# V's tiles on ScalarE's DMA queue, K's on SyncE's, in a decode block whose time is set by the transfers

## The chip, the cores and the metric

The kernel runs on one core of a Trainium2 chip. The metric is the time of one execution on the device in microseconds (us), as the median of several runs of the same program. The engines are named as the profile names them: PE is TensorE (PEld its weight loads), DVE is VectorE, ACT is ScalarE, POOL is GpSimd, SP is SyncE. An engine's name with a q behind it (SPq, ACTq, PEq) is its instruction queue: DMA issues and loop control stand there.

## The reference

One decode step of a transformer block for a batch of 2, one token each: layer norm, attention of 32 heads over a cache of 8192 keys and values, output projection, a second layer norm, and a gated MLP.

```python
def _A_ref(x, k_cache, v_cache, wq, wo):          # x: 2 x 1 x 512; caches: 2 x 32 x 8192 x 128
    q = (x @ wq) ... one row of 128 for each head
    scores = einsum("bhqd,bhkd->bhqk", q, k) * Dh ** -0.5
    o = einsum("bhqk,bhkd->bhqd", softmax(scores), v)
    return o.reshape(B, Sq, Hq * Dh) @ wo
h = x + _A_ref(_layernorm(x), A_k_cache, A_v_cache, A_wq, A_wo)
h2 = h + _B_ref(_layernorm(h), W_gate, W_up, W_down)   # (relu-gated gate * up) @ W_down, F = 1376
```

All inputs are bf16. The two caches are 134 MB each and every byte of them is used once; the weights are some 12 MB.

## The kernel before, in words

The work is cut into N = 32 steps. A step i is one batch element and two heads: its K tile is 128 partitions x 16384 bf16 (4 MB; partitions 0 to 63 hold one head, 64 to 127 the other, 128 keys of 128 numbers in each partition), its V tile has the same shape. K has two buffers (the halves of kbuf), V has two (vbuf0, vbuf1); step i uses buffer i % 2. All engines but GpSimd run in the order in which the program is written (manual_schedule), and waits on semaphores are added for each buffer that is overwritten.

scores(i) writes step i down, and the end of step i - 1 with it:

- VectorE multiplies the K tile in place with the query (L358), folds the 128 products of each key in halves (L383, four adds), sums the last eight (L387), and takes the maximum of each partition (L395).
- TensorE spreads that maximum over the partitions (L397, tile mx). It stands in TensorE's program behind the products of the step before.
- One step later, powers(i): VectorE takes the minimum of the negated maxima (L312), ScalarE the exponentials (L315, two instructions with their accumulators), into pgz.
- values(i): TensorE multiplies pgz with the V tile, 32 products of 128x8 with 128x512: in a hardware loop (L434 to L440) for i < 29, written out (products, L408) for steps 29 and 30, and the other way round (L420, 128 small products) for step 31. Step 30's are cut in two: 24 (FRONT) before the maximum of step 31, 8 behind it.
- collect(i): ScalarE copies the product from PSUM (L450). turn and normalise gather four steps at a time.

So in the order of the program, scores(i) is: the multiply of step i; powers(i - 1); values(i - 1); the loads; collect(i - 1); the folds of step i; the maximum and its matmul.

The loads are in load_kv (L140 to L148, the DMA at L144). Before the steps, SyncE issues Wq, K0 in four pieces, K1 and V0. In scores(i), for i from 1 to 30, it issues K(i + 1), which waits for VectorE to finish step i - 1 in the same buffer, and then V(i), which waits for TensorE to finish the products of step i - 2. A ring is the queue of transfers that one issuing engine has handed to the DMA engines; SyncE's is q1 in the profile, ScalarE's is q10. All loads of the kernel before are in q1, except the two rows of A_x, which ScalarE issues at the very start (L168). single_packet is set for the tiles of steps 1 to 27 (TOGETHER = 28).

Behind the steps SyncE issues V31 (L472), then Wo in three pieces (L480), W_gate and W_up (L489), W_down in three pieces (L493) and its remainder (L498). W_gate, W_up and most of W_down go into K's buffer 0 when step 30 has left it. The second and third piece of W_down wait on SyncE for V30 and for V31 to land, since they use the semaphores of those transfers again, and the remainder waits likewise for the first piece of Wo. After the last step come the output projection (L535), the second layer norm, gate and up (L571), down (L604) and the store (L618).

Of the kernel before, what the change touches and what calls it, by code (L numbers as in the profile page):

```python
# [13 lines left out]
def _free(t, offset, dims):  # L14

    return bass.AP(tensor=t.tensor, offset=t.offset + offset, ap=[t.ap[0]] + [list(d) for d in dims])


def _dram(t, offset, dims):
    return bass.AP(tensor=t.tensor, offset=t.offset + offset, ap=[list(d) for d in dims])  # L20
# [3 lines left out]
def kernel(  # L24
# [13 lines left out]
    nc = tc.nc  # L38
# [53 lines left out]
    vbuf = [big.tile([P, ROW], bf16, name=f"vbuf{s}") for s in range(2)]  # L92
# [44 lines left out]

    FRONT = 24

    def load_kv(cache, buf, i, pieces=1):  # L140
        b, g = steps[i]
        w = ROW // pieces
        for k in range(pieces):
            nc.sync.dma_start(  # L144
                out=buf[i % 2][:, k * w:(k + 1) * w],
                in_=_dram(cache, (b * Hkv + 2 * g) * Sk * Dh + k * w, [[ROW, P], [1, w]]),
                single_packet=0 < i < TOGETHER,
            )  # L148
# [15 lines left out]
    with tc.manual_schedule(engines=ORDERED):  # L164
# [128 lines left out]
        def normalise(i):  # L293
            b, g0, n = divided[i]
            c = slice(2 * g0, 2 * (g0 + n))
            rz = small.tile([P, 2 * NG], f32, tag="rz")
            nc.vector.reciprocal(out=rz[:, c], in_=o_of(i)[:, 1, c])  # L297
            nc.vector.tensor_tensor(out=ocol[:, c, b], in0=o_of(i)[:, 0, c], in1=rz[:, c], op=ALU.mult)
# [6 lines left out]
        def powers(i):  # L305
            b, g = steps[i]
            s = i % 2
            mx_ps, scol = mx.pop(i)
            if i % AGAIN == 0:
                cols["nm"] = small.tile([P, AGAIN, 2], f32, tag="nm", name="nm")  # L310
            nm = cols["nm"][:, i % AGAIN, :]
            nc.vector.tensor_reduce(out=nm, in_=mx_ps, axis=AXIS.X, op=ALU.min)  # L312
            for j in range(2):
                r = slice(j * HALF, (j + 1) * HALF)
                nc.scalar.activation(  # L315
                    out=_free(pgz[s][r, :], j, [[2, NT]]), in_=scol[r, :], func=ACT.Exp, scale=SCALE,
                    bias=nm[r, j:j + 1], accum_out=zc[r, b, g, j:j + 1],
                )

        def scores(i):  # L320
            b, g = steps[i]
            s = i % 2
            kt = kbuf[:, s, :]
            npe = NPE if i == N - 1 else 0
            nmul = NT - npe
            nv = nmul - NACT[i == N - 1]

            if i % AGAIN == 0:
                cols["scol"] = small.tile([P, AGAIN, NT], f32, tag="scol", name="scol")
            scol = cols["scol"][:, i % AGAIN, :]  # L330
            if npe:
                sc_ps = ps.tile([P, NPE, 2], f32, tag="sc")
                kT = small.tile([P, NPE * P], bf16, tag="kT")

                def times_q(c0):
                    for t in range(c0, c0 + TPC):
                        nc.tensor.matmul(
                            out=sc_ps[:, t, :], lhsT=kT[:, t * P:(t + 1) * P], rhs=_free(qT, b, [[B, 2]]),
                            start=True, stop=True,
                        )  # L340

                for c0 in range(0, NPE, TPC):
                    t_ps = ps2.tile([P, TPC, P], bf16, tag="tp")
                    for k in range(TPC):
                        t = nmul + c0 + k
                        nc.tensor.transpose(t_ps[:, k, :], kt[:, t * Dh:(t + 1) * Dh], ident)
                    nc.scalar.activation(
                        out=kT[:, c0 * P:(c0 + TPC) * P], in_=t_ps.rearrange("p t s -> p (t s)"), func=ACT.Copy,
                    )
                    if c0:  # L350
                        times_q(c0 - TPC)
                times_q(NPE - TPC)
                nc.scalar.activation(out=scol[0:HALF, nmul:NT], in_=sc_ps[0:HALF, :, 0], func=ACT.Copy)
                nc.scalar.activation(out=scol[HALF:P, nmul:NT], in_=sc_ps[HALF:P, :, 1], func=ACT.Copy)

            for t0, n in ([(0, NT // 2), (NT // 2, nmul - NT // 2)] if i == 0 else [(0, nmul)]):
                kv = _free(kt, t0 * Dh, [[Dh, n], [1, Dh]])
                nc.vector.tensor_tensor(  # L358
                    out=kv, in0=kv, in1=_free(qrep, (b * NG + g) * Dh, [[0, n], [1, Dh]]), op=ALU.mult,
                )  # L360

            left = waiting[:]
            if i >= 1:
                powers(i - 1)
            if i >= 1:
                values(i - 1)
                tc.no_sync_barrier()
                if i < N - 1:
                    load_kv(A_k_cache, kh, i + 1)
                    load_kv(A_v_cache, vbuf, i)  # L370
            for t in range(nv, nmul):
                whole = small.tile([P, Dh], f32, tag="whole")
                nc.scalar.activation(
                    out=whole, in_=kt[:, t * Dh:(t + 1) * Dh], func=ACT.Copy, accum_out=scol[:, t:t + 1],
                )
            if i >= 1:
                if i < N - 1:
                    collect(i - 1)
            width = Dh
            while width > 8:  # L380
                half = width // 2
                lo = _free(kt, 0, [[Dh, nv], [1, half]])
                nc.vector.tensor_tensor(  # L383
                    out=lo, in0=lo, in1=_free(kt, half, [[Dh, nv], [1, half]]), op=ALU.add,
                )
                width = half
            nc.vector.tensor_reduce(  # L387
                out=scol[:, 0:nv], in_=_free(kt, 0, [[Dh, nv], [1, 8]]), axis=AXIS.X, op=ALU.add,
            )

            for e in left:
                waiting.remove(e)
                normalise(e)
            pm = small.tile([P, 1], f32, tag="pm")
            nc.vector.tensor_reduce(out=pm, in_=scol, axis=AXIS.X, op=ALU.max)  # L395
            mx_ps = ps.tile([P, 2, HALF], f32, tag="mx")
            nc.tensor.matmul(  # L397
                out=mx_ps.rearrange("p a b -> p (a b)"), lhsT=_free(pm, 0, [[0, P]]), rhs=nscale,
                start=True, stop=True,
            )  # L400
            mx[i] = mx_ps, scol
            if 1 <= i < COLS:
                turn(i - 1)
# [10 lines left out]
        def values(i):  # L414
            s = i % 2
            if i >= COLS:
                sums(i)
                g = steps[i][1]
                for t in range(NT):
                    nc.tensor.matmul(  # L420
                        out=o_of(i)[:, 0, 2 * g:2 * g + 2],
                        lhsT=vbuf[s][:, t * Dh:(t + 1) * Dh], rhs=pgz[s][:, 2 * t:2 * t + 2],
                        start=(t == 0), stop=(t == NT - 1),
                    )
                    if t == NT // 2:
                        turn(i - 1)
                return

            made[i] = ps.tile([P, T4 * Dh], f32, tag="po", name="po")
            if i >= LOOPED:  # L430
                products(i, 0, FRONT if i == N - 2 else NT // T4)
                return

            with tc.tile_critical(sync_engine=PE):  # L434
                products(i, 0, LOOP)

                at = {PE: LOOP_AT} if i == 0 else None
                with nc.Fori(1, NT // T4 // LOOP, 1, engines=[PE], head_slot=at) as w:
                    for u in range(LOOP):
                        nc.tensor.matmul(  # L440
                            out=made[i][0:2 * T4, :],
                            lhsT=pgz[s][:, bass.ds((w * LOOP + u) * (2 * T4), 2 * T4)],
                            rhs=vbuf[s][:, bass.ds((w * LOOP + u) * (T4 * Dh), T4 * Dh)],
                            start=False, stop=True, skip_group_check=True,
                        )


        def collect(i):
            _, k = group(i)
            nc.scalar.activation(  # L450
                out=ob[32 * k:32 * k + 2 * T4, :], in_=made.pop(i)[0:2 * T4, :], func=ACT.Copy,
            )
# [14 lines left out]
        for i in range(N - 1):  # L467
            scores(i)
            if i + EARLY < NG // 2:
                make_q(i + EARLY)  # L470
# [176 lines left out]
```

## Time and profile before

| | |
|---|---|
| median of 3 runs | 659.16 us (659.12 to 659.32) |
| profiled execution, first to last instruction (span) | 657.6 us |
| what the median is above that span | 1.5 us |
| VectorE busy | 607.9 us (92%) |
| TensorE busy | 398.7 us (61%) |
| ScalarE busy | 67.0 us (10%) |
| read from HBM | 281.05 MB, 427 GB/s over the span |
| V tile: issue to landing, median | 23.4 us |
| K tile: issue to landing, median | 19.8 us |

The runs are whole executions; the span is that of the one execution that was profiled, and the profile gives no other time for it. A slice row of the page divides the span into 40 equal parts of 16.4 us; a digit is the busy share in tenths. In a timeline a line gives the start and the length in us, the engine, the source line, the operation, the tile written and the tiles read, how many of them were merged, and in brackets how long the engine had been idle and for whom. A landing is the moment at which the last of the 16 DMA engines has reported its share of a transfer. The trace also holds one record for each packet: start, duration, size and queue. A full row of a K or V tile is one such record of 32768 bytes.

### The profile page before, as it was taken

To read this page: it belongs to the slowest core of one execution; us is meant where nothing else is said; L and a number is where in the kernel's file an instruction comes from. 1 tells how busy PE (TensorE), PEld (TensorE's weight loads), DVE (VectorE), ACT (ScalarE), POOL (GpSimd) and SP (SyncE) were. 2 spreads that over 40 slices of the span, in tenths; PEclk is the share of its full clock that TensorE was granted. 3 is DMA by queue.
4 is the path that set the end of the run, shared out by engine and by line. 5 is a ranking of instruction groups with operands and counts; after the bars stand their busy time and mean duration, and the time that the engine had idled before them with its cause. 6 is when DMAs were issued, how large, how long until landed. Compare 5 with 4: busy or idle time off the path is not lost.

```text
span 657.6 us, 7128 instructions
## 1 busy us (share of the span) xinstructions
PE 398.7 (61%) x1647; PEld 129.5 (20%) x1647; DVE 607.9 (92%) x290; ACT 67.0 (10%) x200; POOL 7.9 (1%) x51
## 2 busy tenths in 40 slices
PE   2127666666676555657666556775556665565496
PEld 1002111211121111211112111121112111121256
DVE  0899999999999999999999999999999999999941
ACT  2110111110000000000000000000000000000220
POOL 4000000000000000000000000000000000000000
PEclk9999788798887777898887789767778876779885
DMA  8999999999999999999999999999999999999997
GB/s 359 439 444 421 442 433 427 444 415 446 427 434 433 427 442 425 440 434 427 440 424 441 429 435 432 429 440 424 440 431 432 438 423 441 432 433 436 425 422 298
DMA packets 11379, 281.26 MB, mean 428 GB/s; under 512 B 1282, under 2 KB 1380, under 8 KB 2020
## 3 DMA queue, kind: packets, MB, share of 16 engines
q1 hardware_dynamic: 11360, 281.06, 99.3%
q8 instruction: 9, 0.15, 0.1%
q14 instruction: 6, 0.05, 0.0%
q10 hardware_dynamic: 4, 0.00, 0.0%
HBM read 281.05 MB, written 0.00 MB: 427 GB/s over the span
## 4 chain that ended last, share of the span: by engine, by line
DVE 61%; DMA 36%; PE 1%; issue 1%; SPq 0%; ACT 0%; DVEq 0%; ACTq 0%
DMA kbuf<-in_A_k_cache_dram 30%; DVE kbuf L358 28%; DVE kbuf L383 27%; DVE scol L387 4%; DMA vbuf<-in_A_v_cache_dram 3%; DMA kbuf<-in_B_W_down_dram 3%; PE po L408 1%; DVE nm L312 1%; DVE pm L395 0%; SPq L144 0%; ACT pgz L315 0%; PE d_ps L604 0%; SPq L166 0%; DVE rz L297 0%; PE y_ps L612 0%
## 5 line engine op out<-in xcount | busy, mean ns | idle before, releaser
L440 PE MATMUL po<-vbuf,pgz 128*8 x870 | 300.1, 443 | 68.0 <-issue 66.7
L358 DVE TENSOR_TENSOR kbuf<-kbuf,qrep 128x16384 bf16<-128x16384 bf16 (+2 forms) x33 | 277.1, 8398 | 10.2 <-DMA kbuf<-in_A_k_cache_dram 9.8
L383 DVE TENSOR_TENSOR kbuf<-kbuf 128x8192 bf16<-128x8192 bf16 (+4 forms) x128 | 274.5, 2144 | 3.3
L440 PEld LDWEIGHTS po<-vbuf,pgz 128*8 x870 | 79.9, 92 | 299.1 <-issue 263.9
L408 PE MATMUL po<-vbuf,pgz 128*8 128x512 bf16 x122 | 47.0, 521 | 135.4 <-PEq L434 111.3
L450 ACT ACTIVATE ob<-po 8x512 f32<-8x512 f32 x31 | 18.2, 586 | 436.5 <-PEq L434 427.3
L387 DVE TENSOR_REDUCE scol<-kbuf 128x128 f32<-128x1024 bf16 (+1 forms) x32 | 38.8, 1214 | 1.2
L315 ACT ACTIVATE pgz<-scol,nm 64x128 bf16<-64x128 f32 x64 | 28.0, 438 | 85.4 <-DVE nm L312 84.5
L397 PE MATMUL mx_ps<-nscale,pm 128*128 128x128 f32 x64 | 15.0, 317 | 29.7 <-DVE pm L395 19.0
L408 PEld LDWEIGHTS po<-vbuf,pgz 128*8 128x8 bf16 x58 | 2.7, 84 | 130.4 <-issue 130.4
L397 PEld LDWEIGHTS mx_ps<-nscale,pm 128*128 128x128 f32 x64 | 9.7, 190 | 39.6 <-issue 19.3
L234 PE MATMUL q_ps<-wbig,xn 128*2 128x512 bf16 x32 | 10.7, 469 | 3.0 <-DMA wbig<-in_A_wq_dram 3.0
L315 ACT ACTIVATION_READ_ACCUMULATOR pgz<-scol,nm 64x1 f32 x64 | 11.7, 184 | 0.0
L312 DVE TENSOR_REDUCE nm<-mx_ps 128x2 f32<-128x128 f32 x32 | 9.1, 284 | 1.4 <-PE mx_ps L397 1.4
L408 PEld LDWEIGHTS <-pgz 128*8 128x8 bf16 x64 | 6.1, 98 | 21.3 <-ACT pgz L315 10.0
L395 DVE TENSOR_REDUCE pm<-scol 128x1 f32<-128x128 f32 x32 | 9.1, 286 | 1.1
L459 PE MATMUL o_ps<-sel,ob 128*128 128x8 f32 (+1 forms) x64 | 8.7, 262 | 0.1
L459 PEld LDWEIGHTS o_ps<-sel,ob 128*128 128x128 f32 x64 | 8.0, 197 | 1.4 <-ACT ob L450 1.2
L215 DVE COPY xc<-x_ps 128x8 f32<-128x8 f32 x1 | 0.2, 167 | 8.4 <-PE x_ps L211 8.4
L238 ACT ACTIVATE qrow<-q_ps 2x512 bf16<-2x512 f32 x8 | 4.7, 587 | 29.5 <-PE q_ps L234 29.5
L242 PE MATMUL r_ps<-qrow,pick 2*64 2x256 bf16 x32 | 3.9, 321 | 5.4 <-ACT qrow L238 5.4
L297 DVE RECIPROCAL rz<-o_ps 128x32 f32<-128x32 f32 (+3 forms) x4 | 1.0, 254 | 5.8 <-PE o_ps L289 4.6
(93 smaller groups left out, 75.5 us busy)
## 6 DMA issues: line engine op xcount, KB each, us to landing
vbuf<-in_A_v_cache_dram SPq DMA_DIRECT2D x32, 4096.0 KB, 23.4
kbuf<-in_A_k_cache_dram SPq DMA_DIRECT2D x31, 4096.0 KB, 19.8
wbig<-in_A_wq_dram SPq DMA_DIRECT2D x1, 4096.0 KB, 12.6
kbuf<-in_A_k_cache_dram SPq DMA_DIRECT2D x4, 1024.0 KB, 17.5
wbig<-in_A_wo_dram SPq DMA_DIRECT2D x1, 2048.0 KB, 24.5
wbig<-in_A_wo_dram SPq DMA_DIRECT2D x2, 1024.0 KB, 26.4
kbuf<-in_B_W_gate_dram SPq DMA_DIRECT2D x1, 1376.0 KB, 31.2
kbuf<-in_B_W_up_dram SPq DMA_DIRECT2D x1, 1376.0 KB
```

The costliest lines, as they stand in the source:

```text
L234: nc.tensor.matmul(out=q_ps[0:B, :], lhsT=xn[:, c, :], rhs=wq_sb[:, c, n * 512:(n + 1) * 512], start=(c == 0), stop=(c == KC - 1),)
L312: nc.vector.tensor_reduce(out=nm, in_=mx_ps, axis=AXIS.X, op=ALU.min)
L315: nc.scalar.activation(out=_free(pgz[s][r, :], j, [[2, NT]]), in_=scol[r, :], func=ACT.Exp, scale=SCALE, bias=nm[r, j:j + 1], accum_out=zc ...
L358: nc.vector.tensor_tensor(out=kv, in0=kv, in1=_free(qrep, (b * NG + g) * Dh, [[0, n], [1, Dh]]), op=ALU.mult,)
L383: nc.vector.tensor_tensor(out=lo, in0=lo, in1=_free(kt, half, [[Dh, nv], [1, half]]), op=ALU.add,)
L387: nc.vector.tensor_reduce(out=scol[:, 0:nv], in_=_free(kt, 0, [[Dh, nv], [1, 8]]), axis=AXIS.X, op=ALU.add,)
L395: nc.vector.tensor_reduce(out=pm, in_=scol, axis=AXIS.X, op=ALU.max)
L397: nc.tensor.matmul(out=mx_ps.rearrange("p a b -> p (a b)"), lhsT=_free(pm, 0, [[0, P]]), rhs=nscale, start=True, stop=True,)
L408: nc.tensor.matmul(out=made[i][0:2 * T4, :], lhsT=pgz[s][:, u * 2 * T4:(u + 1) * 2 * T4], rhs=vbuf[s][:, u * T4 * Dh:(u + 1) * T4 * Dh], s ...
L440: nc.tensor.matmul(out=made[i][0:2 * T4, :], lhsT=pgz[s][:, bass.ds((w * LOOP + u) * (2 * T4), 2 * T4)], rhs=vbuf[s][:, bass.ds((w * LOOP ...
L450: nc.scalar.activation(out=ob[32 * k:32 * k + 2 * T4, :], in_=made.pop(i)[0:2 * T4, :], func=ACT.Copy,)
L459: nc.tensor.matmul(out=o_of(i)[:, 0, 2 * g0:2 * (g0 + n)], lhsT=ob[:, t * Dh:(t + 1) * Dh], rhs=sel[:, t, 0:n, :], start=(t == 0), stop=(t ...
```

## The change

load_kv takes the issuing engine as an argument. In the loop V's tiles (V1 to V30) are issued by ScalarE, at the same place of the program: on ScalarE that is behind the exponentials of step i - 1 (L315) and ahead of the copy of step i - 1 (L450). K's tiles, V0, V31 and the weights stay with SyncE.

```diff
-    def load_kv(cache, buf, i, pieces=1):
+    def load_kv(cache, buf, i, pieces=1, by=None):
         b, g = steps[i]
         w = ROW // pieces
         for k in range(pieces):
-            nc.sync.dma_start(
+            (by or nc.sync).dma_start(
                 out=buf[i % 2][:, k * w:(k + 1) * w],
                 in_=_dram(cache, (b * Hkv + 2 * g) * Sk * Dh + k * w, [[ROW, P], [1, w]]),
                 single_packet=0 < i < TOGETHER,
             )
...
                 if i < N - 1:
                     load_kv(A_k_cache, kh, i + 1)
-                    load_kv(A_v_cache, vbuf, i)
+                    load_kv(A_v_cache, vbuf, i, by=nc.scalar)
```

The programs of TensorE and VectorE are the same row for row. ScalarE's has 30 more rows, the V issues; they are gone from SyncE's.

## The prediction

> **What bounds the kernel now.** I read the slices of the page first, then the DMA part, then one period of the loop in the timeline, then the tail.
>
> ```profile
> DVE  0899999999999999999999999999999999999941
> DMA  8999999999999999999999999999999999999997
> GB/s 359 439 444 421 442 433 427 444 415 446 427 434 433 427 442 425 440 434 427 440 424 441 429 435 432 429 440 424 440 431 432 438 423 441 432 433 436 425 422 298
> ...
> q1 hardware_dynamic: 11360, 281.06, 99.3%
> ...
> DVE 61%; DMA 36%; PE 1%; issue 1%; SPq 0%; ACT 0%; DVEq 0%; ACTq 0%
> ```
>
> VectorE and the DMA engines are both full from the second slice to the last two, and one queue, q1 (SP's), carries nearly all bytes. Which of the two decides? A table by stage gives a DMA share of 1.00 and 433 GB/s from 40 to 596 us. The packet records say the same: a row of 32 KB (one partition of a K or V tile) takes 1.213 us, and the next one starts 1.209 us after it on the same engine. A 4 MB tile is 128 rows on 16 engines, 8 each: 8 x 1.209 = 9.67 us. A step moves two tiles: 19.33 us. VectorE's step, from one multiply (L358) to the next, is 19.02 us before 246 us (37.92 to 56.94). So the transfers are the slower of two almost equal chains: VectorE catches up by 0.3 us a step and from 246 us on waits for K, which the chain of waits shows as K transfers. One such period:
>
> ```profile
> 265.95 0.33 SPq L144 DMA_DIRECT2D kbuf<-in_A_k_cache_dram  x1
> 271.71 0.33 SPq L144 DMA_DIRECT2D vbuf<-in_A_v_cache_dram  x1
> 285.19 0.33 SPq L144 DMA_DIRECT2D kbuf<-in_A_k_cache_dram  x1
> 290.94 0.33 SPq L144 DMA_DIRECT2D vbuf<-in_A_v_cache_dram  x1
> ```
>
> ```profile
> 275.89 0.44 ACT L315 ACTIVATE pgz<-scol,nm 64x128 bf16<-64x128 f32 x1
> 276.19 0.18 ACT L315 ACTIVATION_READ_ACCUMULATOR pgz<-scol,nm 64x1 f32 x1
> 291.01 0.59 ACT L450 ACTIVATE ob<-po 8x512 f32<-8x512 f32 x1 [14.63 <-PEq L434]
> ```
>
> ```profile
> 285.84 8.69 DVE L358 TENSOR_TENSOR kbuf<-kbuf,qrep 128x16384 bf16<-128x16384 bf16 x1 [0.36 <-DMA kbuf<-in_A_k_cache_dram]
> ```
>
> K is issued when VectorE has finished with its buffer (265.95), V when TensorE has (271.71). By the records of landings, the V issued before (252.66) lands at 276.09, this K at 285.75, this V at 295.39: one after the other, 9.65 us apart, in the order of issue. K lands just in time: the multiply at 285.84 had waited 0.36 us.
>
> **The change, part by part.**
>
> *Instructions.* 30 V issues (V1 to V30) leave SP's program for ScalarE's; TensorE's and VectorE's programs stay row for row the same. SP gains nothing: V's wait there ends 5.7 us after K's issue, and the next K is due 13.5 us later, so no K stood behind a V. On ScalarE a V issue costs about 0.33 us (SP's row) and stands between the exponentials (L315, done at 276.37) and the copy of L450, which waits 14.6 us for TensorE anyway. Cost: nothing.
>
> *V's issue becomes later.* It now follows the exponentials: 276.4 instead of 271.7, 10.4 us after K's issue instead of 5.8. Cover: this K is served from 276.1 to 285.8, so the engines have 9 us of work. The thinnest cover is at V1: issued near 47.9 (end of the first L315 pair) instead of 38.1, while K2 is served until 52.15. From issue to first packet the first transfer took 1.0 to 1.9 us, so some 2 us remain. If a cover failed, the hole would be lost outright. Value: 0.
>
> *V's new waits* are for the earlier tile of its own buffer, read by TensorE long before, and for TensorE's loop two steps back, which L450 has already waited for. Value: 0.
>
> *Two rings share the engines.* This is what counts, and the kernel before has it only in miniature. (a) The second row of A_x is a ScalarE transfer on queue 10 in the middle of wq's stream: its 1 KB packet was served at 6.405, its closing 4-byte record at 7.656, with one 32 KB row of q1 between. So the rings take turns, row by row. (b) Instruction fetches on queues 8 and 14 cut in the loop's tiles too; where an engine's rows can be followed back, they stood after 1, 3, 4, 5, 6 and 6 of a tile's 8 rows, four of the six in tiles that are marked single_packet. So that mark does not keep a tile together against another ring.
>
> By turns, K no longer waits behind V, nor V behind K: both are in flight most of the time at half speed. The sum of bytes and the rate stay, and some transfer is always open, so the stream as a whole ends when it did. What moves is the order: K and the next V interleave, so at the moment a K lands, part of the V that formerly came after it is already in. Put K's issue at 0, first packet at 1.3, V's first packet at 10.4 + 1.3 = 11.7. The K that paces VectorE must land at about 19.7, so V had half speed for (19.7 - 11.7): 4.0 us of its bytes came ahead of K. **Every K of the transfer-bound stretch therefore lands 4.0 us later than in the serial order**, once, not per step: VectorE runs 4.0 us behind.
>
> *V itself.* With K and V at half speed each while both are open and 9.67 us of service each, K's landing at 19.7 puts V's at 30.1 after K's issue, formerly 29.4 (295.39). TensorE's loop on it starts at 30.9 (296.89), so it is still in time by 0.8 us; if it missed, the matmul behind the loop (mx, ready at 272.3) has 2.7 us more until VectorE's minimum (L312, 274.98). Value: 0; a miss beyond that would be paid only if the engines went idle, and K or V is open then.
>
> *The tail pays the 4.0 us.*
>
> ```profile
> 624.82 7.61 PE L408 MATMUL po<-vbuf,pgz 128*8 128x512 bf16 x24 [6.53 <-DMA vbuf<-in_A_v_cache_dram]
> ...
> 632.88 0.29 DVE L312 TENSOR_REDUCE nm<-mx_ps 128x2 f32<-128x128 f32 x1 [1.37 <-PE mx_ps L397]
> ...
> 634.84 1.77 PE L420 MATMUL o_ps<-pgz,vbuf 128*128 128x2 bf16 x65
> ...
> 653.01 1.01 PE L604 MATMUL d_ps<-hm,kbuf 128*128 128x2 bf16 x32 [0.60 <-DMA kbuf<-in_B_W_down_dram]
> ```
>
> K31 now lands at 615.08, V30 at 624.78, V31 at 634.44. In the new order K31 lands at 619.1; V30 then has 5.66 us left, runs alone for 1.0 us until V31's first packet (its issue follows the products of step 29, near 618.9) and shares the rest: 619.1 + 1.0 + 2 x 4.66 = 629.4. V31 lands at 634.4 as before. The 24 matmuls on V30 start at 629.45 instead of 624.82, so the last exponentials and the values of step 31 move by 4.6 us. Behind them stand 7.5 us of Wo's products, then gate, up and down; there the weights are waited for only 0.15 us (up) and about 0.5 us (down). 4.6 - 0.65 = **+4.0 us**.
>
> *What a change of ring costs.* In (a) q1's row ended at 6.413 and the next began at 6.545: 132 ns for a packet of 46, that is 86 ns for going there and back. In (b) the row behind an 8 KB fetch took 1.455 to 1.753 us instead of 1.213, 0.24 to 0.54 more; a 16 KB fetch cost about 0.8 in all above its size. V has 30 x 8 = 240 rows on each engine: from 0, over 240 x 0.086 = 21 us, to 240 x 0.8 = 190 us. Below nothing: the slowest engine of a tile lands 1.9 us behind the first from 200 us on, after its fetches; that is all two open rings could win back. I take 0 as likeliest, because every foreign packet in the trace was alone and short, and the holes came with the return from it, never on the way in: a row of 32 KB leaves the other ring 1.2 us to get ready. The row nearest in kind (ScalarE's ring into SBUF) gives the upper end of my range.
>
> The Trainium skill (DMA: Bandwidth & Descriptors, Issuing engines are not separate DMA queues) says that DMAs of several issuing engines interleave on the same 16 engines and only issue time is saved: a rule against the change; (a) agrees, and by it the sum of a change of ring would be 0.
>
> **Sum.** The profiled execution spans 657.6 us; the median of the runs is 659.16, 1.5 above it, and I carry the difference over. 659.2 + 4.0 = 663.2, with 661 to 667 for this case alone (lag 2 to 4 us, small costs of changing rings).
>
> **Rivals.**
> 1. *Rings are changed at a price* (22%). 45 to 86 ns per V row: +11 to +21 on top of 4: 674 to 684, worse if the fetches' 0.24 us held. For: every foreign packet left a hole. Against: above.
> 2. *Order unchanged* (14%), not slower. If the engines drain a tile before they turn to the other ring, up to the end, K and V alternate exactly as in the one ring, since each is issued while the other is served: 659.2. It decides at K31: if V30 gets less than about 1.2 us of turns before K31 lands (instead of 8), the tail's 0.65 us hides it. Against: (a) and (b).
> 3. *Whole tiles until step 27, rows after* (8%). load_kv marks steps 1 to 27 as single_packet. V27, marked, would then cut into K28, unmarked, whole: K28 lands 9.67 us late, VectorE cannot recover more than 0.3 a step, less the tail's room of 0.65 to 1: about 668. The Trainium skill (DMA: Bandwidth & Descriptors, Queues, rings and completion order) has engines drain a whole packet before they switch to another ring; the fetches after 1 to 6 rows speak against a packet of a whole tile.
> 4. *The engines gain* (6%): with a second ring always ready, a fetch leaves no hole and the 1.9 us of the slowest engine go: 657.3.
>
> **How the numbers follow.** My own case 50%. Slower by over 0.2% (1.3 us, about what a measurement of this kernel can tell from no change): 50 + 22 + 8 = 80%. Within: 14%. Faster: 6%. The range 658.8 to 685 leaves out rival 4 and the dear end of rival 1.
>
> **What would show it.** Rows of queues 1 and 10 in turn in the packet records; V's issue on ScalarE right behind L315; K and V each 19 to 20 us from issue to landing; VectorE's steps 4 us later than before from some 300 us on; K31 landing near 619, the 24 matmuls of L408 near 629; the DMA share of the loop still 1.00. Rival 1 shows as a period above 19.4 us and less than 433 GB/s; rival 2 as landings of K and V 9.65 us apart with VectorE on its old times; rival 3 as one stall of VectorE at step 28. I am wrong if the engines idle in the loop, or if K, not V, is kept back by more than its half.

## The result, and the profile after

The kernel with two rings takes 661.22 us (median of 5 runs, 660.69 to 661.88), the kernel before 659.12 us beside it (5 runs, 659.07 to 659.32). The ratio is 1.0031, with a 95% interval of 1.002 to 1.0042. The change costs 2.1 us; the forecast was 4.0. The profiled execution took 661.09 us with a span of 659.3 us, 1.7 more than the span of before.

First the slices and the queues of the page of the kernel after:

```profile
DVE  0899999999999999999999999999999999999951
DMA  8999999999999999999999999999999999999996
GB/s 362 435 441 437 423 442 429 432 436 425 437 435 426 441 427 433 437 425 439 433 428 435 431 433 436 427 441 430 428 437 425 441 433 427 439 429 432 437 415 252
...
q1 hardware_dynamic: 7040, 155.23, 54.8%
q10 hardware_dynamic: 4324, 125.83, 44.2%
...
DVE 56%; DMA 40%; PE 3%; issue 1%; SPq 0%; DVEq 0%
```

The bytes are now divided between q1 and q10, and nothing else in the middle has moved: both engines are full and the rate is the same (432.8 GB/s from 40 to 610 us in both kernels, by the packet records). What differs clearly is the last slice, 252 GB/s instead of 298: the stream ends where it did (the last data record at 654.01 us, before 653.93) and the program goes on longer behind it. So the loss is not in the transfers. It is in what is done after them.

The same period as in the prediction, at the end of the loop, in the timeline of after:

```profile
589.03 0.44 ACT L315 ACTIVATE pgz<-scol,nm 64x128 bf16<-64x128 f32 x1 [3.13 <-DVE nm L312]
589.14 0.34 ACTq L144 DMA_DIRECT2D vbuf<-in_A_v_cache_dram  x1
589.55 0.43 ACT L315 ACTIVATE pgz<-scol,nm 64x128 bf16<-64x128 f32 x1
...
598.86 0.33 SPq L144 DMA_DIRECT2D kbuf<-in_A_k_cache_dram  x1
...
618.77 7.63 DVE L358 TENSOR_TENSOR kbuf<-kbuf,qrep 128x14336 bf16<-128x14336 bf16 x1 [0.19 <-DMA kbuf<-in_A_k_cache_dram]
```

V's issue goes out between the two exponentials. K31 is issued at 598.86 and lands at 618.75 (before: 595.19 and 615.08), and VectorE's last multiply follows it at 618.77 instead of 615.10. VectorE still waits only 0.19 us in the step; it is late by 3.5 to 3.9 us, a lag that had built up by about 250 us (247.13 became 251.02) and did not grow any more.

The part of the page on DMA issues (KB each, median us from issue to landing):

```profile
kbuf<-in_A_k_cache_dram SPq DMA_DIRECT2D x31, 4096.0 KB, 19.9
vbuf<-in_A_v_cache_dram ACTq DMA_DIRECT2D x30, 4096.0 KB, 19.9
```

K takes as long as before (19.8), V less (23.4 before), because V is issued 3.9 us later behind K than it was, 9.6 us instead of 5.8. A shorter time from issue to landing is no gain here.

Then the tail, with the line of the kernel before that belongs beside the third one of after:

```profile
632.36 0.49 PE L397 MATMUL mx_ps<-nscale,pm 128*128 128x128 f32 x2
```

```profile
627.75 6.77 PE L408 MATMUL po<-vbuf,pgz 128*8 128x512 bf16 x24 [5.73 <-ACT pgz L315]
634.89 0.29 DVE L395 TENSOR_REDUCE pm<-scol 128x1 f32<-128x128 f32 x1
635.33 0.46 PE L397 MATMUL mx_ps<-nscale,pm 128*128 128x128 f32 x2 [0.81 <-DVE pm L395]
635.82 0.29 DVE L312 TENSOR_REDUCE nm<-mx_ps 128x2 f32<-128x128 f32 x1 [0.64 <-PE mx_ps L397]
637.78 1.77 PE L420 MATMUL o_ps<-pgz,vbuf 128*128 128x2 bf16 x65
...
657.05 0.34 SPq L618 DMA_DIRECT2D out_dram<-y  x1
```

The 24 matmuls start 2.93 us later than before (624.82), the minimum 2.94, the values of step 31 2.94, the store of the output 1.61 (655.44). Look at the releaser of the first line: before it was V's transfer, now it is ScalarE's exponentials. V30 landed at 627.23, half a us before they ended. The releaser of the third line counts for more. Before, the matmul of the last maximum (L397) went out behind the 24 matmuls on V30 without a wait, and VectorE's maximum (L395) had been ready since 631.52. After, the 24 matmuls end only 2.1 us later (634.52 against 632.43), and L397 waits 0.81 us for L395, which starts 3.66 us later than before (631.23). So what sets the end is no longer V30 but VectorE's work on K31.

**Where K31's 3.7 us come from** is seen in the packet records. They carry no engine number, but each record starts within 0.01 us of the end of the one before it on its engine, so they can be put in rows. K and V are rows of 32 KB with their start in us; e is the 4-byte record that closes K31 on that engine and reports it.

```
before, K31's last engine   K609.91 K611.12 K612.33 K613.54 e614.75
after, nine engines like    K610.22 K611.43 V612.64 e613.85 V613.85
after, five engines like    K610.34 K611.55 V612.76 K613.97 V615.18 e616.39
after, two engines, K31's last K610.00 K611.21 V612.42 K613.63 V614.84 K616.05 V617.25 e618.47
```

V30, issued at 608.6, opens on the engines at 612.0 to 613.1. From there an engine serves one row of each ring in turn, and the closing record of 4 bytes takes a turn of its own. An engine that has n rows of K left reports K after n + 1 rows of V: (n + 1) x 1.21 us later. The tile has landed when the last engine has reported, and that one had two rows left: 3 x 1.21 = 3.6 us. Behind K's closing V runs alone. The engines drift apart by this: the first and the last closing record of a K tile lie 0.84 us apart at K2, 2.05, 2.99, 4.05 at the next three, and 4.68 from some 210 us on, with one exception (before: 1.93 at K31). The engine that is behind has more rows left, so it gives more turns away.

### The profile page after: what moved, and what is told of

It is laid out like the page before. It is cut to its first block, busy times and chain, and to the rows that moved or that the text cites. A ratio compares the mean times of both kernels' runs of the same rounds, so it can differ in the third digit from the quotient of the medians.

```text
span 659.3 us, 7101 instructions
## 1 busy us (share of the span) xinstructions
PE 401.8 (61%) x1647; PEld 129.3 (20%) x1647; DVE 608.4 (92%) x290; ACT 66.9 (10%) x200; POOL 7.9 (1%) x51
## 4 chain that ended last, share of the span: by engine, by line
DVE 56%; DMA 40%; PE 3%; issue 1%; SPq 0%; DVEq 0%
DMA kbuf<-in_A_k_cache_dram 40%; DVE kbuf L383 26%; DVE kbuf L358 25%; DVE scol L387 4%; PE att_ps L535 1%; DVE nm L312 1%; PE o_ps L420 1%; PE po L408 0%; DVE pm L395 0%; PE g_ps L571 0%; PE u_ps L571 0%; SPq L144 0%; PE d_ps L604 0%; PE m_ps L157 0%; PE o_ps L459 0%
## 5 line engine op out<-in xcount | busy, mean ns | idle before, releaser
L440 PE MATMUL po<-vbuf,pgz 128*8 x870 | 303.4, 451 | 64.8 <-issue 63.6
L358 DVE TENSOR_TENSOR kbuf<-kbuf,qrep 128x16384 bf16<-128x16384 bf16 (+2 forms) x33 | 277.2, 8399 | 13.6 <-DMA kbuf<-in_A_k_cache_dram 12.9
L450 ACT ACTIVATE ob<-po 8x512 f32<-8x512 f32 x31 | 18.2, 586 | 437.5 <-PEq L434 427.9
L315 ACT ACTIVATE pgz<-scol,nm 64x128 bf16<-64x128 f32 x64 | 28.0, 437 | 86.8 <-DVE nm L312 85.9
L397 PE MATMUL mx_ps<-nscale,pm 128*128 128x128 f32 x64 | 15.0, 317 | 30.3 <-DVE pm L395 19.3
L397 PEld LDWEIGHTS mx_ps<-nscale,pm 128*128 128x128 f32 x64 | 9.7, 191 | 40.2 <-PEq L434 19.4
L315 ACT ACTIVATION_READ_ACCUMULATOR pgz<-scol,nm 64x1 f32 x64 | 11.7, 182 | 0.0
L395 DVE TENSOR_REDUCE pm<-scol 128x1 f32<-128x128 f32 x32 | 9.1, 285 | 1.1
## 6 DMA issues: line engine op xcount, KB each, us to landing
kbuf<-in_A_k_cache_dram SPq DMA_DIRECT2D x31, 4096.0 KB, 19.9
vbuf<-in_A_v_cache_dram ACTq DMA_DIRECT2D x30, 4096.0 KB, 19.9
```

Source lines behind the costliest of these rows:

```text
L315: nc.scalar.activation(out=_free(pgz[s][r, :], j, [[2, NT]]), in_=scol[r, :], func=ACT.Exp, scale=SCALE, bias=nm[r, j:j + 1], accum_out=zc ...
L358: nc.vector.tensor_tensor(out=kv, in0=kv, in1=_free(qrep, (b * NG + g) * Dh, [[0, n], [1, Dh]]), op=ALU.mult,)
L397: nc.tensor.matmul(out=mx_ps.rearrange("p a b -> p (a b)"), lhsT=_free(pm, 0, [[0, P]]), rhs=nscale, start=True, stop=True,)
L440: nc.tensor.matmul(out=made[i][0:2 * T4, :], lhsT=pgz[s][:, bass.ds((w * LOOP + u) * (2 * T4), 2 * T4)], rhs=vbuf[s][:, bass.ds((w * LOOP ...
L450: nc.scalar.activation(out=ob[32 * k:32 * k + 2 * T4, :], in_=made.pop(i)[0:2 * T4, :], func=ACT.Copy,)
```

## The experiments

**The theories.** The *order theory* is the prediction's: the rings change without a price, and what costs is that rows of V come ahead of the end of K. Its rivals: the *ring price* (each V row pays for the change of ring, in all about the 2.1 us measured over 240 rows of an engine) and the *late issue* (V waits behind the exponentials, and that costs by itself). All kernels compute the whole result. In the table a row of 32 KB counts as stretched when it takes over 1.26 us (undisturbed: 1.213); of the 8160 rows 11 are stretched in the kernel before and 11 in the one after, those at instruction fetches. The kernel before took 659.19 to 659.23 us beside these runs.

| kernel | us | ratio (95%) | K31 lands | stretched rows | last data record |
|---|---|---|---|---|---|
| before | 659.12 | | 615.08 | 11 | 653.93 |
| after | 661.22 | 1.0031 (1.002 to 1.0042) | 618.75 | 11 | 654.01 |
| e1_last_only | 664.33 | 1.008 (1.0066 to 1.0094) | 622.12 | 11 | 653.71 |
| e2_to_20 | 659.21 | 1.0001 (0.9992 to 1.001) | 614.90 | 11 | 653.74 |
| e3_early | 902.31 | 1.3684 (1.3662 to 1.3705) | - | 862 | 893.21 |
| e4_unmarked | 661.38 | 1.0035 (1.0021 to 1.0048) | 618.49 | 11 | 653.71 |
| e5_one_ring_late | 660.72 | 1.0024 (1.0015 to 1.0033) | 615.83 | 40 | 654.64 |
| e6_pool | 662.93 | 1.0066 (1.0053 to 1.008) | 621.20 | 71 | 656.65 |
| e7_from_24 | 664.56 | 1.0084 (1.007 to 1.0098) | 621.70 | 58 | 657.49 |
| e8_notes_behind | 659.49 | 1.0005 (0.9996 to 1.0013) | 614.98 | 12 | 653.87 |
| e9_act_later | 665.84 | 1.0086 (1.0064 to 1.0107) | 623.15 | 236 | 661.76 |
| e10_late_from_4 | 660.75 | 1.0023 (1.0014 to 1.0032) | 616.08 | 47 | 654.96 |
| e11_act_later_1 | 661.7 | 1.0034 (1.0021 to 1.0048) | 618.64 | 12 | 653.74 |

### Only the last V tile on the other ring

```diff
-                    load_kv(A_v_cache, vbuf, i, by=nc.scalar)
+                    load_kv(A_v_cache, vbuf, i, by=nc.scalar if i == N - 2 else None)
```

> Only V30, the last of the thirty, goes to ScalarE's queue; V1 to V29 stay on SyncE's. Order theory (the rings take turns row by row, so K lands later by the V rows that are served before it lands; the stream as a whole takes no longer; only the tail pays): V30 arrives while K31 still has some 7 us of rows to go, each of them now alternates with a row of V30, so K31 lands near 622.5 instead of 615.1 and the run takes about 665, 4 us more than with all thirty moved, because no earlier K has been brought forward against a V. Ring-price theory (each V row on the second ring costs something, 2.1 us over 240 rows): 659.2. Late-issue theory (each V issued behind the exponentials costs something): 659.2.

One moved tile costs 5.1 us, more than twice what thirty cost. A price for each row, or for each late issue, would make one tile cost a thirtieth of what thirty cost. Neither can be what the 2.1 us are paid for. The timeline of this kernel:

```profile
604.65 0.36 ACTq L144 DMA_DIRECT2D vbuf<-in_A_v_cache_dram  x1
622.13 7.63 DVE L358 TENSOR_TENSOR kbuf<-kbuf,qrep 128x14336 bf16<-128x14336 bf16 x1 [7.52 <-DMA kbuf<-in_A_k_cache_dram]
631.11 7.21 PE L408 MATMUL po<-vbuf,pgz 128*8 128x512 bf16 x24 [5.51 <-ACT pgz L315]
641.15 1.77 PE L420 MATMUL o_ps<-pgz,vbuf 128*128 128x2 bf16 x65
```

VectorE stands for 7.52 us on K31. V30 is issued at 604.65 while K31, behind V29 in the one ring, has only begun, and the packet records show the turns in full. An engine of those that were last:

```
K607.04 V608.25 K609.46 V610.66 K611.87 V613.08 K614.29 V615.50 K616.71 V617.92 K619.13 V620.34 e621.55
```

Five rows left and the closing record: 6 x 1.21 = 7.3 us; K31 landed 7.0 later than before. VectorE's last multiply starts 7.0 us late, the values of step 31 are 6.3 late, the store (660.27) 4.8.

### Two rings until step 20, one after

```diff
+                    load_kv(A_v_cache, vbuf, i, by=nc.scalar if i <= 20 else None)
```

> V1 to V20 on ScalarE's queue, V21 to V30 on SyncE's as before. Order theory: VectorE is some 3.7 us behind at step 20, then K and V are served one after the other again, K lands on its old times, and VectorE's step of 19.02 us against the transfers' 19.34 wins the lag back by 0.3 us a step, 3.2 us in ten steps; what is left stays inside the tail's room: 659.1 to 659.8. Ring-price theory: 20 of 30 V tiles, 659.1 + 1.4 = 660.5. Late-issue theory: the same 660.5.

Twenty moved tiles cost nothing at all. The chip was on the two rings for two thirds of the loop, VectorE was 3.4 us late at step 20 (405.68 against 402.24), and this is what it did from there, in the timeline:

```profile
405.68 8.69 DVE L358 TENSOR_TENSOR kbuf<-kbuf,qrep 128x16384 bf16<-128x16384 bf16 x1 [0.47 <-DMA kbuf<-in_A_k_cache_dram]
425.00 8.69 DVE L358 TENSOR_TENSOR kbuf<-kbuf,qrep 128x16384 bf16<-128x16384 bf16 x1 [0.21 <-DMA kbuf<-in_A_k_cache_dram]
444.03 8.68 DVE L358 TENSOR_TENSOR kbuf<-kbuf,qrep 128x16384 bf16<-128x16384 bf16 x1
...
577.19 8.68 DVE L358 TENSOR_TENSOR kbuf<-kbuf,qrep 128x16384 bf16<-128x16384 bf16 x1
...
615.53 7.62 DVE L358 TENSOR_TENSOR kbuf<-kbuf,qrep 128x14336 bf16<-128x14336 bf16 x1
```

The first two lines end their wait with a K transfer, the next have no wait: VectorE goes at its own pace, 444.03 to 577.19 in 7 steps of 19.02, 0.3 us a step faster than the transfers. From step 21 to step 31 it wins back 3.0 us; the last multiply is 0.4 us later than before, which the tail hides. So the lag is a matter of order that heals as soon as the order is back; had the rings had a price, it would have been paid by step 20. The cost lies where no step is left to win it back.

### V's issue ahead of the exponentials

```diff
+            if 1 <= i < N - 1:
+                load_kv(A_v_cache, vbuf, i, by=nc.scalar)
...
-                    load_kv(A_v_cache, vbuf, i, by=nc.scalar)
```

> All thirty V on ScalarE's queue, but the issue stands ahead of the exponentials of step i - 1 instead of behind them, so it goes out when TensorE is done with the buffer, near 5.8 us after K's issue as in the kernel before, instead of 9.6. Order theory: the second ring is open about 4 us earlier in each step, so K is served by turns for longer; K31 lands 1 to 1.8 us later than with the change (near 620) and the run takes 662 to 663, worse than the change. Late-issue theory: the issue is as early as before, so the loss goes: 659.2. Ring-price theory: unchanged, 661.2.

This failed as a test. The issue now stands in the program ahead of TensorE's loop, and the loop's entry waits for the transfers written before it, the V just issued among them:

```profile
301.91 1.01 PE L409 MATMUL po<-vbuf,pgz 128*8 128x512 bf16 x2 [12.87 <-DMA vbuf<-in_A_v_cache_dram]
316.14 0.29 DVE L312 TENSOR_REDUCE nm<-mx_ps 128x2 f32<-128x128 f32 x1 [9.25 <-PE mx_ps L398]
328.53 1.02 PE L409 MATMUL po<-vbuf,pgz 128*8 128x512 bf16 x2 [12.42 <-DMA vbuf<-in_A_v_cache_dram]
```

TensorE waits 12.9 and 12.4 us in these two steps, 12.9 in the mean of 29, for a V that it needs a step later, VectorE waits for TensorE, and 902 us say nothing of the rings.

### No tile marked single_packet

```diff
-                single_packet=0 < i < TOGETHER,
+                single_packet=False,
```

> The change as it is, with single_packet off for every tile. Order theory with turns of single rows whatever the mark: the same as the change, 661.2, rows of the two queues alternating alike. If the mark keeps rows of one tile together to some degree against the other ring, the pattern of rows changes: with more turns K lands later in steps 5 to 27, but the last four steps, unmarked already, are the same, and the time moves by less than 1 us.

No difference. With the mark or without it the rings take turns by the row: in the change itself, whose tiles up to step 27 are marked, one engine at 244 us serves K243.32 V244.53 K245.74 V246.95 K248.16 V249.37 e250.58.

### V's issue late in the one ring, and its control

The late issue by itself: the kernel before, with two 4-byte transfers on SyncE ahead of V's issue that read what the exponentials wrote (zc), so that V goes out as late as it does in the change, but in the one ring. In the control they stand behind V's issue.

```diff
                     load_kv(A_k_cache, kh, i + 1)
+                    bp, gp = steps[i - 1]
+                    for j in range(2):
+                        r = slice(j * HALF, j * HALF + 1)
+                        nc.sync.dma_start(out=note[r, :], in_=zc[r, bp, gp, j:j + 1])
                     load_kv(A_v_cache, vbuf, i)          # in e8 ahead of the notes
```

> One ring, as in the kernel before, but V's issue on SyncE waits for the exponentials of step i - 1 (two transfers of 4 bytes each, that read what the exponentials have written, stand ahead of it), so it goes out some 4.6 us later than before, a little later even than with the change. Order theory: K is being served at that time, so nothing moves: K31 lands at 615 and the run takes 659.2 to 659.6. Late-issue theory (the change lost its 2.1 us because V's issue stands behind the exponentials): 661.2.

> A control for the one-ring run with the late V, which came out at 660.7, 1.5 us over the kernel before, with every transfer of its last stretch 0.75 us later and K and V still in their old order. Here the same two transfers of 4 bytes a step wait for the same exponentials, but stand behind V's issue, so V goes out as early as in the kernel before. Order theory: the 1.5 us are the price of the 60 small transfers (they all run on one DMA engine) and not of V's lateness, so it is the same here: 660.4 to 661.0. Late-issue theory: V is early again: 659.2.

The late issue costs 1.5 us, against my expectation of at most 0.4. The control costs 0.3, where the expectation for the order theory was the whole 1.5; the late-issue theory's 659.2 came closer. K31 lands at 615.83, 0.75 us later, as much as the whole stream, so the order is not moved. What is lost is DMA time: the last data record ends 0.7 us later, and 40 rows are stretched. V1 is issued at 48.57, K2's rows end on the engines from 51.0 us on, and on some of them the first row of V1 starts only at 52.2: 27 rows between 51 and 58 us are stretched. The profiled execution, at 660.35, was 1.1 above the kernel before; 0.7 of the stream and 0.3 of the notes are nearly all of it.

> The one-ring run with the late V again, but late only from step 4 on. In the first such run the packet records show 28 stretched rows and a hole of the engines between 50 and 55 us and none behind it: V1, issued at 48.6, came too late for the engines that had finished K2 at 51.3. So if lateness costs only where the engines run dry, V1 to V3 on their old times leave nothing of the 1.5 us but the 0.3 of the small transfers: 659.2 to 659.7. If lateness itself costs in every step: 660.6.

Expected was that the loss goes when steps 1 to 3 are left alone. It did not: 660.75 is what the late-issue theory gave (660.6). Of the 47 stretched rows 35 lie between 109 and 149 us, behind V4, V5 and V6, which go out 11.6 to 13.0 us behind K, while the first engines have ended K 14.5 to 15.4 us after its issue. Behind 200 us only rows at instruction fetches are stretched, with V some 11.4 us behind K. The last data record ends 1.0 us late; with the 0.3 of the notes that is the 1.3 by which its profiled execution is above the kernel before. So the late issue has a price of its own where the engines run dry, and my "thinnest at V1" was not the whole of it. In the change no row but those at instruction fetches is stretched: V1 goes out at 47.07, 1.5 us sooner than in e5.

### V by the third issuing engine

```diff
+                    load_kv(A_v_cache, vbuf, i, by=nc.gpsimd if i >= 2 else None)
```

> V2 to V30 on GpSimd's queue, V1 on SyncE's: again a second ring, but on an engine that has nothing else to do, so V's issue goes out when TensorE is done with the buffer, near 5.8 us after K's, as in the kernel before. It replaces the run with the early issue, in which TensorE's loop waited for the V tile that was written just ahead of it. Order theory: the second ring is open up to 4 us earlier in each step, K is served by turns for longer, K31 lands near 620 and the run takes 662 to 663, unless GpSimd takes some us to put the transfer together, which brings it back towards 661. Late-issue theory: 659.2. If this queue's packets are cut otherwise, the turns may be unequal.

```profile
601.36 0.33 SPq L144 DMA_DIRECT2D kbuf<-in_A_k_cache_dram  x1
607.99 0.53 POOL L144 DMA_DIRECT2D vbuf<-in_A_v_cache_dram  x1 [18.79 <-PEq L434]
621.22 7.63 DVE L358 TENSOR_TENSOR kbuf<-kbuf,qrep 128x14336 bf16<-128x14336 bf16 x1 [0.22 <-DMA kbuf<-in_A_k_cache_dram]
```

GpSimd runs nothing here that holds the issue, so V goes out 6.6 us behind K instead of 9.7, more of K is left when V opens (most engines report K31 after three or four V rows, formerly one to three) and K31 lands 6.1 us late. Earlier is worse, as the order theory says. But 71 rows are stretched in this kernel, and its stream ends 2.7 us late, so part of the 3.7 us may not be the order.

### Two rings only from step 24 on

```diff
+                    load_kv(A_v_cache, vbuf, i, by=nc.scalar if i >= 24 else None)
```

> V24 to V30 on ScalarE's queue, V1 to V23 on SyncE's. Order theory: at the first steps of the second ring VectorE still runs on the old times, V arrives with much of K left, and K lags by some 7 us; with each further step the lag shrinks by VectorE's 0.3 us until it meets the 3.7 us of the full change. So seven tiles moved cost more than thirty, and less than one: K31 near 617 to 618 after a stall of about 7 us at step 25, VectorE behind by about 5 at the end, the run 663.0 to 663.8. Ring-price theory: 659.2 + 0.5. Late-issue theory: the same.

```profile
479.61 8.69 DVE L358 TENSOR_TENSOR kbuf<-kbuf,qrep 128x16384 bf16<-128x16384 bf16 x1 [0.26 <-DMA kbuf<-in_A_k_cache_dram]
506.23 8.69 DVE L358 TENSOR_TENSOR kbuf<-kbuf,qrep 128x16384 bf16<-128x16384 bf16 x1 [7.44 <-DMA kbuf<-in_A_k_cache_dram]
515.38 0.36 ACTq L144 DMA_DIRECT2D vbuf<-in_A_v_cache_dram  x1
```

Seven tiles cost 5.4 us, more than thirty: the first V on the other ring throws K back by 7.4, as in e1. The expected size was 1 us too small (663.0 to 663.8), and K31 lands at 621.70 instead of 617 to 618, for a reason that I had not thought of. VectorE's stall makes the next exponentials late and with them V25's issue (515.38), while V24 had landed by 511.5 and K26 ends on the engines from 515.9 on. K27, which waits for VectorE too, goes out at 525.04, and V25 ends from 526.7 on. At both places the engines run dry, 58 rows are stretched and the stream ends 3.6 us late.

### V's issue still later

```diff
                     load_kv(A_k_cache, kh, i + 1)
+                    if i >= 4:                                  # e11: i >= 8, one copy
+                        for _ in range(3):
+                            nc.scalar.activation(out=idle, in_=_free(ones, 0, [[0, 8], [1, P]]), func=ACT.Copy)
                     load_kv(A_v_cache, vbuf, i, by=nc.scalar)
```

> The change, with V issued later still: from step 4 on three idle copies of 128x1024 stand on ScalarE between the exponentials and V's issue, 2 to 3 us more. Order theory: V's first row is served later, so fewer rows of V get in ahead of K; the lag of VectorE shrinks from 3.7 us by half of the delay, to 2.2 to 2.7, K31 lands near 617.5 instead of 618.7, and the run is faster than the change: 660.0 to 660.8, if V still lands in time for TensorE's loop. Late-issue theory: another 2 to 3 us of lateness cost as much again as the first 4 did in proportion: 662.3 or more. Ring-price theory: 661.2.

> The change with one idle copy instead of three on ScalarE ahead of V's issue, from step 8 on: some 1.3 us later than with the change. With three copies the first engines had finished K before V's rows came, 221 rows of V were stretched and the stream ended 7.7 us late. With one copy V's issue, near 11 us after K's, still comes 4 us ahead of the first engine's end of K (15.3): order theory without holes gives a lag smaller by half of 1.3 and 660.4 to 661.2. If engines run dry already at this delay, the time rises above 661.5. Late-issue theory: 662.

With three idle copies ahead of it, V should open when hardly any of K is left, and the order theory alone expected a gain. The page of that kernel and its timeline:

```profile
GB/s 364 446 424 437 439 430 410 414 422 410 422 430 421 431 426 414 431 435 428 433 411 420 430 434 426 433 433 433 432 428 431 433 437 428 430 437 432 433 417 283
```

```profile
391.43 0.33 SPq L145 DMA_DIRECT2D kbuf<-in_A_k_cache_dram  x1
401.57 3.23 ACT L373 ACTIVATE idle<-ones 128x1024 bf16<-128x1024 f32 x3
403.75 0.34 ACTq L145 DMA_DIRECT2D vbuf<-in_A_v_cache_dram  x1
```

V goes out 12.3 us behind K here and up to 15.4 in other steps, and the first engines finish K some 15 us after its issue: the engines wait, slices fall to 410 GB/s, and the stream ends 7.8 us late (its six runs lie between 661.91 and 667.27). The four steps in which V is 14.4 us or more behind K hold 101 of the 236 stretched rows. The time lies where the late-issue theory put it (662.3 or more), by way of engines that run dry. Whether there is a delay between "too early, K is put back" and "too late, the engines run dry" stays open: behind 250 us no step of a two-ring run had V between 10 and 12.3 us behind K. One copy was too little to tell: in e11 the issue went out 9.5 us behind K, as in the change, because ScalarE's queue issues it at 588.71 while the copy ahead of it starts at 589.72. No version beat the kernel before; e2 equals it.

## Why the prediction was right, step by step, and where its sizes were off

1. *Bound by the transfers, VectorE 0.3 us a step faster.* Confirmed by e2, where VectorE without a wait goes 19.02 us a step and wins back 3.0 us in ten steps.
2. *Moving the issues to ScalarE costs nothing, and SyncE gains nothing.* Right. They went out even before the second exponential, 9.6 us after K's issue rather than 10.4.
3. *The later issue is covered.* Right in the change (11 stretched rows in both kernels, the stream's end unmoved), but by less than worked out. From issue to first row I had put 1.0 to 1.9 us, from the first transfer of all, which met idle engines. Here it is 3.2 to 4.0: V1, issued at 47.07, starts at 51.07, just as the first engine ends K2's rows; on another engine a row of K2 still went ahead of it at 50.70. e5 shows what 1.5 us more did to one ring. "Some 2 us remain" was wrong: at most 0.4 remained.
4. *V's new waits cost nothing.* No wait of ScalarE for a V buffer shows.
5. *The rings take turns row by row.* Confirmed on every engine. The Trainium skill (DMA: Bandwidth & Descriptors, Queues, rings and completion order) has an engine drain a whole packet, typically 9 to 17 descriptors, before it goes to another ring. In this trace the turn is one record, be it a 32 KB row or the closing 4 bytes, in marked and unmarked tiles (e4); if a record is a descriptor, which no run here shows, the trace differs. Rivals 2 and 3 (whole tiles) fall with that.
6. *K lands 4.0 us later, once.* Measured 3.7 at K31, nearly constant from about 250 us on. The size was nearly right, but not by the way it was worked out: "both are in flight most of the time at half speed" was wrong. V opens at 13.1 us (issue 9.6 and 3.5 to the first row) and not at 11.7, and when it does most engines have only K's closing record left. The half-speed formula would give (19.9 - 13.1) / 2 = 3.4. What sets the landing is the last engine and the turn of the closing record: three turns of 1.21. I had left out both, and they nearly made up for the V that opens later: that 4.0 came so near 3.7 is partly luck.
7. *V lands in time.* Right: in the loop TensorE waits for no V.
8. *The tail pays 4.0.* This is the mis-sized term, and its path was wrong too. V30 was to land at 629.4, and through its 24 matmuls the values of step 31 were to move by 4.6; they moved by 2.94. V31's first row comes 3.6 us after its issue (622.26 after 618.62), so V30 has the engines alone until then and lands at 627.23. Its 24 matmuls end 2.1 us later than before and no longer decide. VectorE's chain behind K31 does: its last maximum (L395) is 3.66 us later. Before, this maximum was ready 0.84 us ahead of its matmul on TensorE (631.52 and 632.36); after, the matmul follows it by 0.15. So 0.69 is absorbed: 3.66 - 0.69 = 2.97. Behind this the tail's room is 1.3 us (2.94 - 1.61), not 0.65: Wo's last products are 2.65 us later than before, those of up 2.35, those of down 2.00, the store 1.61. In the kernel before the last products of down waited for W_down's third piece (654.23), and the room lay further back than the two waits that I added up. e1 agrees: 7.0 late at VectorE's last multiply, 6.3 at the values, 4.8 at the store, and there too the last maximum's matmul waits for VectorE (0.38 us).
9. *Changing rings costs 0.* Right: no row of K or V is stretched by a change (e1: strict turns through a whole tile, 11 stretched rows as before), the period is 19.36 us and the rate 432.8 GB/s. The Trainium skill (DMA: Bandwidth & Descriptors, Issuing engines are not separate DMA queues) says that transfers of several issuers share the same 16 engines and interleave; the trace agrees, and the equal rate is what that leaves. Rival 1 (674 to 684) and rival 4 (a fetch that leaves no hole) fall: the fetches stretch 11 rows in both.

The sum by the measured terms: 3.66 - 0.69 - 1.33 = 1.6 us at the store, against 1.7 of the two spans and 2.1 of the medians; the five runs of the change spread from 660.69 to 661.88. So direction and mechanism of the lag were right, and the loss came out at about half of the forecast, because the tail absorbs more than was put down for it.

What stays open: what part of e6 is the order and what the dry engines, and whether the 3.2 to 4.0 us to the first row come from rows that the engine has already taken on, or from the issue. One row speaks for the first: in e7, V25, issued at 515.38, has its first row at 516.37, 1.0 us later, when the first engines had just ended K26.

## What to carry to other kernels

A second ring added nothing here, where the engines are full (433 GB/s with one and with two); it only changed what comes first, and a row that comes earlier is paid for by the transfer that the bound engine waits for. The price is paid once, so look for the place where no step is left to win it back: here the first twenty tiles are free, because ten steps win their lag back, and the last one alone costs 5.1 us. If the order of landings matters, keep it in one ring, and issue each transfer well before the engines run out: V1 went out 4.0 us ahead in the change, which was enough, and 2.4 ahead in e5, which was not.

## What the runs showed of the hardware that was not expected

- The closing record of a transfer, 4 bytes, waits for a turn like a row of 32 KB: engines that had finished K's rows reported them 1.21 us later because of it.
- Turns drive the engines apart: 1.9 us between the first and the last engine of a K tile in one ring, 4.7 in two.
- From issue to the first row, V's transfers took 3.2 to 4.0 us on engines that are busy with the other ring; Wq's, on idle engines at the start, took 1.0 to 1.9.
- Where engines had run dry, the next rows took longer: up to 2.2 us in e5 and 2.8 in e7 instead of 1.213.
- ScalarE's DMA issue is not held until the instruction written before it has run: at 589.14 it went out ahead of the exponential that starts at 589.55, and in e11 a whole us ahead of the copy (588.71 and 589.72).
